# Attention and FFN in one kernel: lending two idle PSUM banks to the score tiles

## The chip, the cores and the metric

The kernel runs on one core of one Trainium2 chip. The metric is the device time of one execution in microseconds. The engines are named as in the profile: PE (TensorE), DVE (VectorE), ACT (ScalarE), POOL (GpSimd), SP (SyncE, which issues most DMAs here).

## The reference

Eight batches, eight heads, 576 positions, head size 64: causal attention with a learnt forgetting bias, then a feed-forward network with 2048 inner columns over the joined heads.

```python
scores = scale * np.matmul(q, k.transpose(0, 1, 3, 2))
s_pos = np.maximum(s, 0.0)
cum = np.cumsum(s_pos, axis=-1)
bias = -(cum[:, :, :, None] - cum[:, :, None, :])
scores = np.where(causal, -1000000000.0, scores + np.minimum(bias, 0.0))
scores = scores - np.max(scores, axis=-1, keepdims=True)
attn = np.exp(scores)
attn = attn / (np.sum(attn, axis=-1, keepdims=True) + 1e-09)
attn_out = np.matmul(attn, v)                  # (8, 8, 576, 64)
...
x = np.ascontiguousarray(attn_out.transpose(0, 2, 1, 3)).reshape(B * S, H * D)
h = x @ w_in
g = np.where(pos, h, np.where(neg, 0.0, (h + beta) ** 2 / (4.0 * beta)))
return (g @ w_out).astype(np.float32)
```

The weights come as 64-bit floats, which the kernel decodes itself on the chip.

## The kernel before, in words

Two streams of work share the engines. The first is attention. A job is a pair of heads and one half of the positions: half 0 has columns 0 to 319 (query tiles 0, 1 and 2), half 1 has columns 320 to 575 (query tiles 3 and 4). Eight jobs make a batch: four pairs in half 0, then four in half 1. A job has six score tiles. Each takes its PSUM bank from the pool `ps_s` (two banks), is written by one or two matmuls (line 407 for the first eight jobs, lines 412 and 413 later) and is emptied by one DVE instruction (line 418) that adds the mask and finds the extreme of each row. ACT then takes the exponential (line 429); once both heads of a query tile are there, `weights_t` normalises them into P, split into a high and a low 16-bit part, on ACT, POOL and DVE (lines 445 to 456), and a DMA issued by SP transposes them (line 457). `att_out` multiplies with V (line 475) into a tile px, which takes a bank of the same pool `ps_s`; ACT and DVE empty it into x (lines 486 and 487). Ahead of a job's scores stands a preparation of Q and K (lines 352 to 362) into buffers of which there is one each.

The second stream is the feed-forward network, half by half: a first half of 320 columns and a second of 256 for each batch, 16 steps each. `ffn_h` makes one tile h (line 530, twelve matmuls over the four pairs' x, two banks in `ps_h`), from which ACT, DVE and POOL make g in two parts (lines 542 to 557). `ffn_y` multiplies g with w_out into four accumulating tiles y of 128 output rows each (line 569, twelve matmuls a step), over all 16 steps. Each y tile has a bank of its own, tags y0 to y3 in `ps_y`; at the last step ACT scales it into a tile o and a DMA stores it (lines 583 and 584). So all eight banks are given away: two for scores and px, two for h, four for y. In a second half a y tile fills 256 of its bank's 512 columns.

At the start the weights are decoded, 16 chunks of w_in and 16 of w_out: the load (line 189), ACT and DVE instructions on the raw bits (lines 198 to 215) and a PE matmul that sums the exponents' bounds (line 203, tiles sum_wi in the banks y0 to y3, sum_wo in y0 and y1), then the scaling and splitting (lines 228 to 236). w_in comes with the first four attention jobs; w_out in the shadow of the first FFN half, whose h tiles are made ahead and whose y are made in two pairs of tiles (lines 652 to 658).

The program's order is written by the loop at its end, with attention six jobs ahead of the FFN later on. But the tile framework's scheduler places instructions anew when the kernel is built, by priorities and by its own estimate of when operands and buffers are free. A tile that finds no free buffer waits in that schedule too, and others are placed ahead of it. So the number of banks changes the order on every engine.

Of the kernel before, what the change touches and what calls it, by code (L numbers as in the profile page):

```python
# [9 lines left out]
F32 = mybir.dt.float32  # L10
# [4 lines left out]
AF = mybir.ActivationFunctionType  # L15
# [56 lines left out]
def attention_ffn(ctx: ExitStack, tc: tile.TileContext, qT, kT, vT, s, w_in, w_out, yT):  # L72
# [311 lines left out]

    vbs = {}

    ttr = [None]
    late = []

# [2 lines left out]
    def scores(n, i, hd, c0, c1):  # L392
# [8 lines left out]
            pbs[n, i].append(Pt)  # L401
            G.memset(Pt[:R, W:W + D], 0.0)
        Pt = pbs[n, i][hd]
        sc = ps_s.tile([P, 512], F32, tag="s", name=f"s{n}_{i}_{hd}_{c0}")
        j = jobs.index((n, i // 3))
        if j < F32_JOBS:
            T.matmul(
# [56 lines left out]
    def att_out(n, hf):  # L464

        b, p = n // NPAIR, n % NPAIR
        h_off, N, tiles = HALF[hf]
        nj = tiles[-1] + 1
        PT, VT = pts_.pop((n, hf)), vts[n]
        px = ps_s.tile([P, 512], F32, tag="s", name=f"px{n}_{hf}")  # L470
        steps = [(j, vl, pl) for j in range(nj) for vl, pl in ((0, 0), (1, 0), (0, 1))]
        for m, (j, vl, pl) in enumerate(steps):
            lo = max(0, j * P - h_off)
            for hd in range(2):
                T.matmul(  # L475
                    px[hd * D:(hd + 1) * D, lo:N],
                    VT[:, vl * NB + j, hd * D:(hd + 1) * D],
                    PT[:, 4 * j + 2 * hd + pl, lo:],
                    start=(m == 0), stop=(m == len(steps) - 1),
                )  # L480
        if p == 0:
            X[b, hf] = gp.tile([P, NKT, 2, N], F16, tag=f"x{hf}", bufs=2, name=f"x{b}_{hf}")
        x = X[b, hf]
        e = exs[b][:, p:p + 1]
        with tc.high_priority(offset=X_LEAD):
            A.activation(x[:, p, 0], px[:, :N], AF.Copy, scale=e)  # L486
            V.scalar_tensor_tensor(x[:, p, 1], px[:, :N], e, x[:, p, 0], ALU.mult, ALU.subtract)
# [68 lines left out]
                A.copy(g[:, 0], u)  # L556
            G.tensor_tensor(g[:, 1], u, g[:, 0], ALU.subtract)  # L557

    ys = {}

    def ffn_y(b, hf, ft, g, ms=tuple(range(NKT))):
        h_off, N, _ = HALF[hf]
        if ft == 0:
            for m in ms:
                ys[b, hf, m] = ps_y.tile([P, 512], F32, tag=f"y{m}", name=f"y{b}_{hf}_{m}")
        for m in ms:
            c0 = ft % 2 * 2 * P + m % 2 * P
            for n, (wl, gl) in enumerate(((0, 0), (1, 0), (0, 1))):
                T.matmul(  # L569
                    ys[b, hf, m][:, :N], WO[8 * (m // 2) + ft // 2][:, wl, c0:c0 + P], g[:, gl],  # L570
                    start=(ft == 0 and n == 0), stop=(ft == NFT - 1 and n == 2),
                )
        if ft == NFT - 1:
            last = (b, hf) == (B - 1, len(HALF) - 1)
            for m in ms:
                tag, bufs = ("u", 4) if last and m >= 2 else ("o", O_BUFS)
                o = gp.tile([P, N], F32, tag=tag, bufs=bufs, name=f"o{b}_{hf}_{m}")
                y = ys[b, hf, m][:, :N]
                with tc.high_priority(offset=FFN_LEAD):
                    if last and m % 2:  # L580
                        V.tensor_scalar(o, y, ysc[b][m // 2], None, ALU.mult)
                    else:
                        A.activation(o, y, AF.Copy, scale=ysc[b][m // 2])
                (nc.sync if last and m % 2 else nc.scalar).dma_start(
                    yT[m * P:(m + 1) * P, b * S + h_off:b * S + h_off + N], o
                )

    def ffn_step(s, k):

# [22 lines left out]
                batch_scales_v(0)  # L612
    while late:
        late.pop(0)()
    V.tensor_reduce(a_in, w1.bound, axis=AX, op=ALU.max)
    batch_scales(0)
    for c in range(3):
# [75 lines left out]
```

## Time and profile before

| what | value |
|---|---|
| median of three runs | 1115.04 us (1110.25 to 1115.35) |
| the profiled execution | 1111.73 us |
| its span, first to last instruction | 1109.9 us |
| PE busy | 1010.8 us, 91% |
| DVE, ACT, POOL busy | 76%, 65%, 61% |
| matmuls of h and of y | 3072 each |
| mean granted TensorE clock | 0.963 |

Lines of groups read: line, engine, operation, out<-in, shapes, count, then busy us, mean ns of one, and the idle time of the engine ahead of them with what ended it. Lines of stretches read: from and to in us, length, then busy us and count for PE, PE's weight loads, DVE, ACT and POOL, the granted clock, the DMA share and GB/s. Lines of waits read: who waits for whom, us in total, times, longest.

### The profile page before, as it was taken

The numbers are of one execution on the slowest core, as the hardware profiler recorded it, in microseconds if no ns is written. First come the engines' busy times: TensorE is split into PE (matmuls) and PEld (weight loads), VectorE is DVE, ScalarE is ACT, GpSimd is POOL, SyncE is SP. The second block draws the span as 40 slices with busy tenths as digits, with TensorE's granted clock in tenths as the row PEclk, the third lists the DMA queues.
The fourth block names the chain that finished last, engine by engine and source line by source line (L and its number), as shares of the span: only waits on it lengthen the run. The fifth ranks groups of instructions, "written<-read, shape, count | busy, mean of one in ns | idle before, by whom it ended". The sixth has DMA issues, their size and how long they took to land.

```text
span 1109.9 us, 25082 instructions
## 1 busy us (share of the span) xinstructions
PE 1010.8 (91%) x8495; PEld 774.9 (70%) x8496; DVE 846.3 (76%) x2325; ACT 725.8 (65%) x1703; POOL 679.0 (61%) x1173
## 2 busy tenths in 40 slices
PE   2456898799999999999999999899999999899998
PEld 1232466587768877777778877687778877787787
DVE  7887966688787877787778877787777887887533
ACT  4765985677567774867567765777576765777432
POOL 4782795775556764766467664666476665765522
PEclk9955999799999999999999999999999999999999
DMA  7876653786468663886468763877387763676300
GB/s 235 218 200 192 170 87 91 158 173 155 100 122 188 148 152 71 187 162 158 79 146 177 161 136 81 177 160 163 68 176 155 165 137 74 158 156 138 68 25 19
DMA packets 340775, 155.01 MB, mean 140 GB/s; under 512 B 290856, under 2 KB 322472, under 8 KB 340648
## 3 DMA queue, kind: packets, MB, share of 16 engines
q1 hardware_dynamic: 330944, 143.49, 59.6%
q10 hardware_dynamic: 9704, 9.93, 2.9%
q8 instruction: 67, 1.10, 0.4%
q14 instruction: 60, 0.49, 0.1%
HBM read 72.31 MB, written 9.73 MB: 74 GB/s over the span
## 4 chain that ended last, share of the span: by engine, by line
PE 61%; DVE 12%; POOL 8%; DMA 7%; issue 6%; ACT 5%; ACTq 0%; SPq 0%; DVEq 0%; POOLq 0%
PE y L569 25%; PE h L530 25%; PE px L475 4%; DMA pt<-pb 3%; PE s L412 3%; PE s L413 3%; DVE pb L456 2%; ACT u L542 2%; POOL pb L453 2%; POOL pb L450 2%; DVE p L418 1%; DVE Q L357 1%; DMA vt<-vb 1%; POOL vb L371 1%; DVE h L545 1%
## 5 line engine op out<-in xcount | busy, mean ns | idle before, releaser
L530 PE MATMUL h<-x,WI 128*128 128x256 f16 (+1 forms) x3072 | 463.9, 290 | 7.4 <-ACT x L486 3.4
L569 PE MATMUL y<-g,WO 128*128 128x256 f16 (+1 forms) x3072 | 457.8, 288 | 7.0 <-POOL g L557 5.3
L530 PEld LDWEIGHTS <-WI 128*128 128x128 f16 x3072 | 291.1, 99 | 97.0 <-issue 13.9
L569 PEld LDWEIGHTS <-WO 128*128 128x128 f16 x3072 | 288.1, 98 | 92.9 <-issue 13.8
L557 POOL TENSOR_TENSOR g<-u,g 128x320 f16<-128x320 f32 (+1 forms) x256 | 206.0, 805 | 152.1 <-ACT g L556 151.6
L429 ACT ACTIVATE p<-p,mn 64x64 f32<-64x64 f32 (+4 forms) x320 | 179.4, 561 | 142.7 <-DVE mn L418 122.2
L542 ACT ACTIVATE u<-h,ub,us 128x320 f32<-128x320 f32 (+1 forms) x256 | 149.1, 583 | 120.3 <-PE h L530 115.3
L545 DVE SCALAR_TENSOR_TENSOR h<-h,ws,u 128x320 f32<-128x320 f32 (+1 forms) x256 | 132.4, 517 | 110.6 <-ACT u L542 108.1
L450 POOL TENSOR_SCALAR pb<-p,rs 64x128 f16<-64x128 f32 (+4 forms) x160 | 95.3, 596 | 171.2 <-DVE rs L446 112.1
L453 POOL TENSOR_TENSOR pb<-p,pb 64x128 f16<-64x128 f32 (+4 forms) x160 | 173.9, 1087 | 9.5
L456 DVE SCALAR_TENSOR_TENSOR pb<-p,rs,pb 64x128 f16<-64x128 f32 (+4 forms) x160 | 134.6, 841 | 47.1 <-POOL pb L450 47.0
L418 DVE CUSTOM_DVE_ANT_0 p<-s,mask 64x64 f32<-64x64 f32 (+4 forms) x320 | 134.4, 420 | 31.3 <-PE s L413 23.0
L412 PE MATMUL s<-K,Q 128*64 128x64 f32 (+1 forms) x336 | 126.2, 377 | 16.0 <-DVE mn L418 10.9
L546 DVE SCALAR_TENSOR_TENSOR u<-u,r,h 128x320 f32<-128x320 f32 (+1 forms) x256 | 130.3, 509 | 6.8 <-DVE h L545 0.5
L451 ACT ACTIVATE p<-p,rs 64x64 f32<-64x64 f32 (+4 forms) x160 | 89.6, 560 | 51.3 <-DVE rs L446 49.4
L556 ACT CAST g<-u 128x320 f16<-128x320 f32 (+1 forms) x256 | 107.9, 421 | 10.3 <-DVE u L546 10.3
L413 PE MATMUL s<-K,Q 68*64 68x64 f32 (+1 forms) x336 | 102.8, 307 | 2.1 <-DMA K<-cumd 1.3
L452 POOL TENSOR_SCALAR pb<-p 64x128 f16<-64x128 f32 (+4 forms) x160 | 93.2, 583 | 11.9 <-ACT p L451 11.0
L475 PEld LDWEIGHTS <-vt 128*64 128x64 f16 x1536 | 73.4, 113 | 36.7 <-issue 30.2
L475 PE MATMUL px<-pt,vt 128*64 128x256 f16 (+3 forms) x1536 | 83.5, 259 | 13.3 <-DMA pt<-pb 8.7
L412 PEld LDWEIGHTS s<-K,Q 128*64 128x64 f32 (+1 forms) x336 | 61.5, 183 | 27.3 <-DVE mn L418 8.2
L413 PEld LDWEIGHTS s<-K,Q 68*64 68x64 f32 (+1 forms) x336 | 61.9, 184 | 5.8 <-issue 1.7
(105 smaller groups left out, 983.0 us busy)
## 6 DMA issues: line engine op xcount, KB each, us to landing
rk<-in_k_dram SPq DMA_DIRECT2D x56, 288.0 KB
v<-in_v_dram SPq DMA_DIRECT2D x32, 288.0 KB
rq<-in_q_dram SPq DMA_DIRECT2D x56, 160.0 KB
rk<-in_k_dram SPq DMA_DIRECT2D x56, 160.0 KB
wir<-in_moe_w_in_dram SPq DMA_DIRECT2D x16, 512.0 KB
wor<-in_moe_w_out_dram SPq DMA_DIRECT2D x16, 512.0 KB
rq<-in_q_dram SPq DMA_DIRECT2D x56, 128.0 KB
out_dram<-o ACTq DMA_DIRECT2D x32, 160.0 KB
```

What stands on the lines that cost most here:

```text
L412: T.matmul(sc[:R, :c1 - c0], Q1[:, hd, qo:qo + R], K1[:, hd, c0:c1], start=True, stop=False)
L413: T.matmul(sc[:R, :c1 - c0], Q2[:KC, hd, qo:qo + R], K2[:KC, hd, c0:c1], start=False, stop=True)
L418: ttr[0] = V.tensor_tensor_reduce(out=Pt[:R, c0:c1], in0=sc[:R, :c1 - c0], in1=mask[:R, mo:mo + c1 - c0], scale=-0.125 if j < F32_JOBS els ...
L429: A.activation(Pt[:R, :W], Pt[:R, :W], AF.Exp, bias=m2[:R], scale=-1.0, accum_out=sums[n, i][:R, hd:hd + 1])
L453: G.tensor_tensor(los[1], pw, his[1], ALU.subtract)
L456: V.scalar_tensor_tensor(los[0], pv, rs[:R, :1], his[0], ALU.mult, ALU.subtract)
L475: T.matmul(px[hd * D:(hd + 1) * D, lo:N], VT[:, vl * NB + j, hd * D:(hd + 1) * D], PT[:, 4 * j + 2 * hd + pl, lo:], start=(m == 0), stop=( ...
L530: T.matmul(h[:, :N], WI[4 * kt + ft // 4][:, wl, ft % 4 * P:(ft % 4 + 1) * P], x[:, kt, xl], start=(n == 0), stop=(n == 3 * NKT - 1),)
L542: first = A.activation(u, h[:, :N], AF.Relu, bias=ubi[b], scale=usc[b][:, fg:fg + 1]).ins
L545: V.scalar_tensor_tensor(h[:, :N], h[:, :N], wsc[b][:, fg:fg + 1], u, ALU.mult, ALU.max)
L557: G.tensor_tensor(g[:, 1], u, g[:, 0], ALU.subtract)
L569: T.matmul(ys[b, hf, m][:, :N], WO[8 * (m // 2) + ft // 2][:, wl, c0:c0 + P], g[:, gl], start=(ft == 0 and n == 0), stop=(ft == NFT - 1 an ...
```

## The change

In a second half, two y tiles of 256 columns share one bank: the tiles m = 0 and 1 lie in y0, the tiles 2 and 3 in y1. Only the first matmul of the first tile carries the start flag, and the second tile's first matmul is kept behind it (`issue_after`). At the end of the half one copy of 512 columns and one store of two tiles take the place of two each; in the very last half ACT copies the first bank and DVE the second.

The banks y2 and y3 are then free in second halves. A flag, `spare`, lends them to score and px tiles: every other such tile goes to `ps_y` under tag y2 or y3 in turn, the others to `ps_s` as before. The flag goes up when the decoding of w_in has been issued, down when the first half of a batch opens its tiles 2 and 3, and up again at the end of that half. So four banks serve the score and px tiles from there to the first half's second pair of y tiles, and in all second halves. The first halves' y tiles keep a bank each.

```diff
+    spare, turn = [False], [0]
+
+    def s_tile(name):
+        turn[0] += 1
+        if spare[0] and turn[0] % 2:
+            return ps_y.tile([P, 512], F32, tag=f"y{2 + turn[0] // 2 % 2}", name=name)
+        return ps_s.tile([P, 512], F32, tag="s", name=name)
...
-        sc = ps_s.tile([P, 512], F32, tag="s", name=f"s{n}_{i}_{hd}_{c0}")
+        sc = s_tile(f"s{n}_{i}_{hd}_{c0}")
...
-        px = ps_s.tile([P, 512], F32, tag="s", name=f"px{n}_{hf}")
+        px = s_tile(f"px{n}_{hf}")
...
+        w = 1 + hf
         if ft == 0:
-            for m in ms:
-                ys[b, hf, m] = ps_y.tile([P, 512], F32, tag=f"y{m}", name=f"y{b}_{hf}_{m}")
+            if ms[-1] == NKT - 1 and not hf:
+                spare[0] = False
+            for m in ms[::w]:
+                ys[b, hf, m // w] = ps_y.tile([P, 512], F32, tag=f"y{m // w}", name=f"y{b}_{hf}_{m}")
...
-                T.matmul(
-                    ys[b, hf, m][:, :N], WO[8 * (m // 2) + ft // 2][:, wl, c0:c0 + P], g[:, gl],
-                    start=(ft == 0 and n == 0), stop=(ft == NFT - 1 and n == 2),
-                )
+                opens = ft == 0 and n == 0
+                with tc.issue_after(opened[0]) if opens and m % w else ExitStack():
+                    opened[0] = T.matmul(
+                        ys[b, hf, m // w][:, m % w * N:(m % w + 1) * N],
+                        WO[8 * (m // 2) + ft // 2][:, wl, c0:c0 + P], g[:, gl],
+                        start=(opens and m % w == 0), stop=(ft == NFT - 1 and n == 2 and m % w == w - 1),
+                    ).ins
...
-                    if last and m % 2:
-                        V.tensor_scalar(o, y, ysc[b][m // 2], None, ALU.mult)
+                    if on_v:
+                        V.tensor_scalar(o.rearrange("p m n -> p (m n)"), y, scale, None, ALU.mult)
...
+            if ms[-1] == NKT - 1 and not hf:
+                spare[0] = True
...
     while late:
         late.pop(0)()
+    spare[0] = True
```

In the rows of instruction lists below, lines from 407 on carry the changed kernel's numbers where the list is of the change: 412 and 413 are 420 and 421 there, 475 is 483, 530 is 538, 569 is 582, 457 is 465. The names are s (scores: query tile, head, first column), px, h and y (half, then step or output tile), and a number for the buffer.

More of the change, by code (lines that the diff above doesn't have):

```diff
@@ L557, in g_split @@
             G.tensor_tensor(g[:, 1], u, g[:, 0], ALU.subtract)
-    ys = {}
+    ys, opened = {}, [None]
     def ffn_y(b, hf, ft, g, ms=tuple(range(NKT))):
         h_off, N, _ = HALF[hf]
+        w = 1 + hf
         if ft == 0:
-            for m in ms:
-                ys[b, hf, m] = ps_y.tile([P, 512], F32, tag=f"y{m}", name=f"y{b}_{hf}_{m}")
+            if ms[-1] == NKT - 1 and not hf:
+                spare[0] = False
+            for m in ms[::w]:
+                ys[b, hf, m // w] = ps_y.tile([P, 512], F32, tag=f"y{m // w}", name=f"y{b}_{hf}_{m}")
         for m in ms:
@@ L568, in ffn_y @@
             for n, (wl, gl) in enumerate(((0, 0), (1, 0), (0, 1))):
-                T.matmul(
-                    ys[b, hf, m][:, :N], WO[8 * (m // 2) + ft // 2][:, wl, c0:c0 + P], g[:, gl],
-                    start=(ft == 0 and n == 0), stop=(ft == NFT - 1 and n == 2),
-                )
+                opens = ft == 0 and n == 0
[5 more added lines that the diff above has]
+                    ).ins
         if ft == NFT - 1:
             last = (b, hf) == (B - 1, len(HALF) - 1)
[L575 to L578, printed above, removed]
+            for m in ms[::w]:
+                on_v = last and m > 0
+                o = gp.tile([P, w, N], F32, tag="o", bufs=O_BUFS, name=f"o{b}_{hf}_{m}")
+                y, scale = ys[b, hf, m // w][:, :w * N], ysc[b][m // 2]
                 with tc.high_priority(offset=FFN_LEAD):
-                    if last and m % 2:
-                        V.tensor_scalar(o, y, ysc[b][m // 2], None, ALU.mult)
-                    else:
-                        A.activation(o, y, AF.Copy, scale=ysc[b][m // 2])
-                (nc.sync if last and m % 2 else nc.scalar).dma_start(
-                    yT[m * P:(m + 1) * P, b * S + h_off:b * S + h_off + N], o
-                )
+                    if on_v:
+                        V.tensor_scalar(o.rearrange("p m n -> p (m n)"), y, scale, None, ALU.mult)
+                    else:
+                        A.activation(o.rearrange("p m n -> p (m n)"), y, AF.Copy, scale=scale)
+                (nc.sync if on_v else nc.scalar).dma_start(
+                    yT[m * P:(m + w) * P, b * S + h_off:b * S + h_off + N].rearrange("(m p) n -> p m n", p=P), o
+                )
+            if ms[-1] == NKT - 1 and not hf:
+                spare[0] = True
     def ffn_step(s, k):
```

## The prediction

> **What bounds the kernel now.** I read the page first, for the engine that is full and the stretches in which it is not.
>
> ```profile
> span 1109.9 us, 25082 instructions
> PE 1010.8 (91%) x8495; PEld 774.9 (70%) x8496; DVE 846.3 (76%) x2325; ACT 725.8 (65%) x1703; POOL 679.0 (61%) x1173
> ...
> PE   2456898799999999999999999899999999899998
> ...
> PEclk9955999799999999999999999999999999999999
> ```
>
> TensorE is full from the ninth slice on, so the end moves only by what PE loses: idle time and a lowered clock. To see where, I cut the start into stages and then took six stretches of 40 us, those in which a batch passes from its 320-column half to its 256-column half (the last row is their sum), and at last the time between them.
>
> ```profile
> 60.00:125.00 65.00, 44.23 (x186) 23.94 (x186) 54.30 (x147) 45.95 (x91) 36.95 (x58) 0.60 0.68 181
> 125.00:188.00 63.00, 59.57 (x432) 40.05 (x433) 45.31 (x118) 44.91 (x88) 46.37 (x58) 0.97 0.54 108
> 188.00:214.00 26.00, 15.08 (x124) 11.30 (x121) 17.34 (x55) 16.23 (x46) 18.71 (x35) 0.74 0.77 156
> 214.00:320.00 106.00, 105.63 (x930) 83.60 (x929) 84.18 (x233) 69.55 (x165) 67.83 (x115) 1.00 0.60 129
> ```
>
> ```profile
> 320.00:360.00 40.00, 36.63 (x338) 30.16 (x336) 31.77 (x103) 29.77 (x86) 27.65 (x65) 0.96 0.84 190
> ...
> 560.00:600.00 40.00, 37.44 (x342) 30.44 (x341) 31.11 (x98) 28.98 (x83) 28.63 (x62) 0.96 0.81 171
> ...
> 800.00:840.00 40.00, 37.51 (x338) 29.82 (x336) 30.46 (x101) 28.47 (x77) 25.25 (x53) 0.96 0.71 154
> ...
> sum 240.00, PE 222.45 PEld 180.26 DVE 187.32 ACT 174.57 POOL 161.22; mean PE 37.07 PEld 30.04 DVE 31.22 ACT 29.10 POOL 26.87
> ```
>
> ```profile
> sum 520.00, PE 516.33 PEld 403.29 DVE 400.29 ACT 333.83 POOL 303.45; mean PE 86.05 PEld 67.21 DVE 66.72 ACT 55.64 POOL 50.58
> ```
>
> The first numbers after a stretch are its length and PE's busy time; the one after the five engines is the granted clock. So PE idles 20.8 us in 60 to 125, when the weights are decoded, 3.4 in 125 to 188, 10.9 in 188 to 214, 17.6 in the six passages (240 − 222.45) and only 3.7 in the 520 us between them. The clock costs a little more: a stretch of 40 us at 0.96 lost 1.6 us, and three show it: 4.8. Behind 214 there are thus some 22 us to be had in the passages, and hardly anything elsewhere.
>
> What PE waits for comes from the list of waits, for 214 to 1080, and for 188 to 214:
>
> ```profile
> PE s L412 <- DVE mn L418: 7.0, 9, 1.9
> PE y L569 <- POOL g L557: 5.3, 7, 1.3
> PE s L412 <- DVE Q L357: 4.2, 5, 1.5
> ```
>
> ```profile
> PE px L475 <- DMA pt<-pb: 4.5, 1, 4.5
> PE s L412 <- DVE mn L418: 3.9, 3, 1.8
> ```
>
> "PE s <- DVE mn" is a score matmul whose bank is not free yet: VectorE's reduction at line 418 has to empty one of the two. That is 7.0 of the 22 us by name. The 4.5 us belong to one place, which the chain of waits tells step by step:
>
> ```profile
> 188.95 0.87 DVE rs L445
> ...
> 190.40 0.77 ACT p L451
> 191.24 1.28 POOL pb L452
> 192.59 2.18 POOL pb L453
> 194.91 5.58 DMA pt<-pb
> 200.62 2.77 PE px L475 x30
> ```
>
> From the last scores of batch 0's fourth pair to its px matmuls lie over 11 us of other engines' work, and PE has nothing else left to do: the half that comes next needs that px.
>
> **The change, part by part.** *More banks let scores move ahead.* The scheduler places a tile when its bank is free, so the list of the program is another one. First place: PE, where batch 0 goes over to its second half; px_1 on pt_1_1661 is the fourth pair's, h_1_0 the next half's first tile. Before:
>
> ```order
> L412 MATMUL s_1_1_0_1934<-K_1825,Q_1824 128x192
> L413 MATMUL s_1_1_0_1934<-K_90,Q_89 128x192
> L412 MATMUL s_2_0_0_1963<-K_1825,Q_1824 128x320
> L413 MATMUL s_2_0_0_1963<-K_90,Q_89 128x320
> L412 MATMUL s_2_1_0_1973<-K_1825,Q_1824 128x320
> L413 MATMUL s_2_1_0_1973<-K_90,Q_89 128x320
> L475 LDWEIGHTS vt_668
> L475 MATMUL px_1_1987<-pt_1_1661,vt_668 64x256
> ```
>
> After, the place where the last of those scores went, and what stands ahead of the px:
>
> ```order
> L582 MATMUL y_0_2_1752<-g_0_12_1390,WO_145 128x320
> L420 MATMUL s_2_1_0_1973<-K_1825,Q_1824 128x320
> L421 MATMUL s_2_1_0_1973<-K_90,Q_89 128x320
> L582 LDWEIGHTS WO_145
> L582 MATMUL y_0_3_1753<-g_0_12_1390,WO_145 128x320
> ```
>
> ```order
> L538 MATMUL h_1_0_2045<-x_1_1361,WI_122 128x256
> L538 LDWEIGHTS WI_114
> L538 MATMUL h_1_1_2077<-x_1_1361,WI_114 128x256
> L483 LDWEIGHTS vt_668
> L483 MATMUL px_1_1987<-pt_1_1661,vt_668 64x256
> ```
>
> The next job's scores moved from right ahead of the px into the first half's y matmuls. Between the pair's last scores (s_4_1_288) and its px stood 8 FFN matmuls, 30 of px and 12 of scores; now 111 FFN matmuls and the same others. An FFN matmul's price comes from the chain:
>
> ```profile
> 1099.46 1.31 PE y L569 x12
> ...
> 146.90 1.63 PE h L530 x12
> ```
>
> That is 0.109 us at 256 columns and 0.136 at 320: 103 matmuls more, most at 320, are some 14 us of cover for a chain of 11.7 (188.95 to 200.62). So the 4.5 us go, and the score waits beside them (3.9), since those scores stand among y matmuls now. Of 188 to 214 I take 10 us off: the 10.9 idle, less 2, and 1 for the clock (0.74 there). Bounds: 4 (the score waits alone) to 15 (all idle, and 4 for the clock).
>
> Second place: PE in the passages, here batch 4. Before, the second 320-column pair's scores:
>
> ```order
> L530 MATMUL h_1_1_10268<-x_1_9179,WI_126 128x256
> L412 MATMUL s_0_1_0_10041<-K_1825,Q_1824 64x64
> L413 MATMUL s_0_1_0_10041<-K_90,Q_89 64x64
> L412 MATMUL s_1_0_0_10077<-K_1825,Q_1824 128x192
> L413 MATMUL s_1_0_0_10077<-K_90,Q_89 128x192
> L530 LDWEIGHTS WI_126
> L530 MATMUL h_1_0_10222<-x_1_9179,WI_126 128x256
> ```
>
> After:
>
> ```order
> L582 MATMUL y_0_2_9315<-g_0_12_9955,WO_144 128x320
> L420 MATMUL s_0_1_0_10009<-K_1825,Q_1824 64x64
> L421 MATMUL s_0_1_0_10009<-K_90,Q_89 64x64
> L582 LDWEIGHTS WO_144
> L582 MATMUL y_0_3_9316<-g_0_12_9955,WO_144 128x320
> ```
>
> The pair's six score tiles stood among 27 FFN matmuls, 3.3 us; now among 73, about 9 us, and the px that the second half's first tile needs comes ahead of that half instead of behind its ninth matmul. It stays so in every later batch. What is late next: the third pair's six tiles stand closer (72 matmuls become 36, at least 3.9 us), but they have four banks; and the Q preparation (line 357, 4.2 us) is untouched. I keep 4.2 and some 4 more of the 22, so 14 go. Bounds: 7 (only the waits named mn) to 22.
>
> I weigh a rule against this. *By the rows above 7.0 us are put down to banks, the rest to other releasers.* The Trainium skill, "TensorE: Matmul & The Clock Gate", section "HAM oscillation — how this bites in real kernels", reports of its kernel that "adding PSUM double-buffering gave no further gain". By that, banks would return nothing here; what that makes of the time is the first rival.
>
> *The weights chain.* The same freedom puts attention ahead of w_out's decoding. Third place: SP's queue (wor = raw w_out chunks). Before:
>
> ```order
> L189 DMA wor_971<-in_moe_w_out_dram 128x2x512
> L189 DMA wor_978<-in_moe_w_out_dram 128x2x512
> L189 DMA wor_1155<-in_moe_w_out_dram 128x2x512
> L189 DMA wor_1162<-in_moe_w_out_dram 128x2x512
> L321 DMA QF_93<-in_q_dram 64x2x256
> L189 DMA wor_1209<-in_moe_w_out_dram 128x2x512
> ```
>
> After:
>
> ```order
> L189 DMA wor_971<-in_moe_w_out_dram 128x2x512
> L321 DMA QF_93<-in_q_dram 64x2x256
> L321 DMA KF_94<-in_k_dram 64x2x576
> L465 DMA_TRANSPOSE pt_1_944<-pb_3_945 128x16x128
> L189 DMA wor_978<-in_moe_w_out_dram 128x2x512
> ```
>
> Six of the 16 chunks now stand behind a P transpose whose input VectorE must finish, and three such transposes are ahead of the last chunk; it was one chunk and one transpose. On VectorE six more score reductions, two more P residuals and some small instructions stand ahead of the last decode (line 215):
>
> ```profile
> L418 DVE CUSTOM_DVE_ANT_0 p<-s,mask 128x448 f32<-128x448 f32 x64 | 39.4, 616 | 6.7 <-PE s L413 4.9 <-PE s L407 1.2 <-POOL pb L453 0.5
> L456 DVE SCALAR_TENSOR_TENSOR pb<-p,rs,pb 128x640 f16<-128x640 f32 x32 | 37.8, 1181 | 0.0
> L456 DVE SCALAR_TENSOR_TENSOR pb<-p,rs,pb 128x512 f16<-128x512 f32 x32 | 36.1, 1128 | 11.9 <-POOL pb L450 11.9
> L418 DVE CUSTOM_DVE_ANT_0 p<-s,mask,mn 128x288 f32<-128x288 f32 x64 | 32.4, 506 | 2.1 <-PE s L413 1.4 <-PE s L407 0.5
> ```
>
> Two at 0.62, four at about 0.5, 1.18 and 1.13 are 5.5 us; with the small ones about 7.5. VectorE idled 10.7 us in 60 to 125 and 17.7 in 125 to 188, so most of it can fill holes: I take +2. Bounds: −6 (PE's 20.8 idle us fill, and GpSimd's work comes earlier) to +8, unless the queue blocks: second rival.
>
> *Two tiles in a bank, the end.* Half as many copies of 512 columns instead of 256, off the path except at the end:
>
> ```profile
> 1101.91 4.09 PE L569 MATMUL y<-g,WO 128*128 128x256 f16 x36
> ...
> 1105.83 0.88 DVE L581 TENSOR_SCALAR o<-y,ys 128x256 f32<-128x256 f32 x2 [1.98 <-PE y L569]
> ```
>
> VectorE's two copies took 0.88 us, from before PE's end at 1106.0; one copy of 512 columns has the same elements but cannot start before the bank's last matmul, so +0.1 to +0.5, and a store of twice the bytes: I take +0.5 (0 to +1). The Trainium skill, "PSUM — Partial Sum Buffer", section "PSUM bank collisions raise a hardware error", says that no two engines may touch one bank's quadrant at once; so a copy waits for both tiles of its bank, not for its own. By that the price here is the upper end, +0.5 for the copy; no row of this trace has two tiles in a bank. Where the banks are handed back, y_0_2 and y_0_3 wait for a reduction (0.6 us), with over 3 us of other matmuls since the bank's last score in the list: nothing.
>
> The sum, against the profiled execution's own 1111.7 us (span 1109.9 and 1.8 around it; 3.3 under the median of the runs, 1115.04): 1111.7 − 10 − 14 + 2 + 0.5 = 1090.2.
>
> **The rivals.** *Banks were not the bound.* Two thirds of the passages' waits bear other names, and the transposed DMA remains. Then the next wait comes up where one is removed and only little is left: 1111.7 − 4 + 2 = 1110, no change. Against it: the list moves the consumer, not the bank alone. 0.11.
>
> *The weights come late.* Two transposes more stand ahead of the last wor load. If each holds SP's queue for its whole chain, 10.1 us from line 451 to the landing by the rows above (190.40 to 194.91 + 5.58), the last decode comes 20.2 + 7.5 = 27.7 us later, and with it PE's last sum matmul of the weights, now at
>
> ```profile
> 138.74 0.39 PE sum_wo L203
> ```
>
> The first half's y must follow it. With the 188 to 214 stall gone (−10) and only the named bank waits in the passages (−7), the time is 1111.7 + 27.7 − 10 − 7 = 1122.4: slower. It decides once that matmul is more than 17 us later, at 156. Against it: VectorE's holes, and ten chunks whose place in the queue is unchanged. 0.06.
>
> *Half of it.* 188 to 214 improves by its score waits alone (4), the passages by 7, the weights cost 2: 1103. It is the forecast's weak end, 0.13.
>
> **How the numbers follow.** My forecast, 1090, has 0.70. Its own ends: −15 −22 −6 gives 1069, −4 −7 +8 +1 gives 1109.7; ends that need every term at its bound together are unlikely, so I cut to 1076 below and 1106 above, which leaves out the rivals that are not faster and about 3 in 100 below. A measurement of this kernel tells about 0.5% from no change: faster is under 1109.5, against the median. Forecast and weak end give faster 0.83, the first rival 0.11 same, the second 0.06 slower.
>
> **What would show it.** Right: the px of batch 0's fourth pair without a wait of microseconds, PE idle in each passage under 1.5 us (2.9 now), the clock at 1.00 in the stretches of 0.96, the waits "PE s <- DVE mn" behind 214 near nothing. Wrong: the last sum_wo matmul behind 150, or passages as idle as now under other releasers' names (POOL g, DVE Q), or a new idle stretch where the third 320-column pair's scores stand close.

## The result and the profile after

The changed kernel takes 1107.82 us (median of 8 runs, 1101.69 to 1114.57); the kernel before, run beside it, 1113.54 us (8 runs, 1109.87 to 1115.79). The ratio is 0.9947, with a 95% interval of 0.9924 to 0.9971: faster by about half a per cent, 5.7 us. The forecast was 1090, with a range up to 1106, so the time lies 17.8 us above the forecast and outside the range.

The profiled execution of the changed kernel took 1112.35 us, one of its longer ones, so it says where time went rather than how much. Its page:

```profile
span 1110.6 us, 24982 instructions
PE 1012.2 (91%) x8495; PEld 781.6 (70%) x8496; DVE 851.8 (77%) x2324; ACT 725.1 (65%) x1688; POOL 692.8 (62%) x1173
...
PE   2466899899999999999999899999999999989998
...
PEclk9955899999999999999999999999999999999999
```

PE's seventh and eighth slices, 8 and 7 before, are 9 and 8 now. The stages of the start, in the columns of the prediction (length, PE, PEld, DVE, ACT, POOL, granted clock, DMA share, GB/s):

```profile
60.00:125.00 65.00, 45.27 (x165) 24.06 (x167) 52.77 (x152) 41.64 (x86) 37.85 (x62) 0.55 0.74 187
125.00:188.00 63.00, 60.24 (x439) 40.34 (x438) 49.84 (x130) 51.87 (x103) 53.60 (x65) 0.96 0.55 114
188.00:214.00 26.00, 21.44 (x197) 17.62 (x196) 18.61 (x54) 17.11 (x47) 18.35 (x37) 0.93 0.80 178
214.00:320.00 106.00, 102.85 (x897) 80.44 (x896) 85.31 (x232) 70.19 (x162) 67.46 (x114) 0.98 0.65 129
```

In 188 to 214 PE is busy 21.44 us instead of 15.08, with 197 matmul records instead of 124. Then the sums over the six passages, and over the 520 us between them:

```profile
sum 240.00, PE 232.70 PEld 191.52 DVE 200.02 ACT 183.57 POOL 172.78; mean PE 38.78 PEld 31.92 DVE 33.34 ACT 30.60 POOL 28.80
```

```profile
sum 520.00, PE 502.12 PEld 395.11 DVE 388.59 ACT 320.13 POOL 298.66; mean PE 83.69 PEld 65.85 DVE 64.77 ACT 53.35 POOL 49.78
```

This is the main part of the miss. The passages did gain, most of the 14 us that were forecast: PE's busy time rose from 222.45 to 232.70, 10.3 us. But between them it fell from 516.33 to 502.12, 14.2 us. The waits of 214 to 1080 name what came:

```profile
PE px L483 <- DMA pt<-pb: 17.8, 10, 2.9
PE s L420 <- DVE x L495: 2.2, 4, 1.5
...
PE s L420 <- DVE Q L357: 1.1, 1, 1.1
...
PE y L582 <- POOL g L565: 0.8, 3, 0.5
```

The bank waits named mn ("PE s <- DVE mn", 7.0 us before) are gone, and Q (4.2) and g (5.3) have shrunk to 1.1 and 0.8. In their place PE stands 17.8 us before px matmuls whose transposed P has not landed (0.8 us before). Of these, 11.7 us fall on one px of a batch, that of the first pair in the 256-column half's attention (up to 2.9 us in each of the batches 2 to 7), and 5.4 on the fourth 320-column pair's (batches 1 to 3).

**Why P is late.** One such place in full, that first pair in batch 4. SP's queue and PE:

```profile
619.36 2.95 SPq L465 DMA_TRANSPOSE pt<-pb  x1
```

```profile
607.99 0.30 PE L421 MATMUL s<-K,Q 68*128 68x288 f32 x1
...
625.53 1.87 PE L483 MATMUL px<-pt,vt 128*64 128x256 f16 x15 [2.73 <-DMA pt<-pb]
```

The pair's last score ends at 608.3, its transpose is issued 11.1 us later, and px starts another 6.2 us on, after 2.73 us of idling. Between the score and the transpose stands first VectorE:

```profile
607.97 1.15 DVE L464 SCALAR_TENSOR_TENSOR pb<-p,rs,pb 128x512 f16<-128x512 f32 x1 [0.33 <-POOL pb L458]
609.04 0.47 DVE L554 SCALAR_TENSOR_TENSOR u<-u,r,h 128x256 f32<-128x256 f32 x1
609.44 0.51 DVE L426 CUSTOM_DVE_ANT_0 p<-s,mask,mn 128x288 f32<-128x288 f32 x1
...
609.87 0.45 DVE L426 CUSTOM_DVE_ANT_0 p<-s,mask 128x288 f32<-128x288 f32 x1
...
610.47 0.52 DVE L426 CUSTOM_DVE_ANT_0 p<-s,mask,mn 128x288 f32<-128x288 f32 x1
```

Three score tiles that PE wrote between 605.5 and 608.3 lie in their banks until VectorE takes them at 609.4 to 611.0, one right after the other: ahead of them stand the residual of the tile before (1.15 us, after a wait of 0.33 for GpSimd's line 458) and a step of the FFN. So the last score and its reduction are 2.5 us apart, from start to start. In the kernel before they are 0.7 us apart, and the transpose comes 8.2 us after the end of the score (619.63 to 627.79):

```profile
619.34 0.29 PE L413 MATMUL s<-K,Q 68*128 68x288 f32 x1
```

```profile
620.02 0.51 DVE L418 CUSTOM_DVE_ANT_0 p<-s,mask,mn 128x288 f32<-128x288 f32 x1
```

```profile
627.79 2.93 SPq L457 DMA_TRANSPOSE pt<-pb  x1
```

Of the 2.9 us by which the transpose is later, 1.8 thus arise ahead of the reduction. The rest arises behind it: the tile's exponential stands behind ScalarE's preparation of Q and K and starts 2.6 us after the reduction's start (610.47 to 613.08), where it was 1.3 (620.02 to 621.36).

So two more banks let PE hand in its scores early, but the engines behind them don't work faster: a wait of PE for a bank became a wait of the scores in a bank, and PE met the same delay at px. Worked out from the same rows for six jobs of batch 4 (us from the end of the job's last score matmul to the issue of its last transpose, and from there to px):

| | 320 columns: pair 1 | 2 | 3 | 4 | 256 columns: pair 1 | 2 |
|---|---|---|---|---|---|---|
| before | 7.5, 7.5 | 11.1, 4.8 | 8.0, 6.2 | 9.3, 5.4 | 8.2, 7.2 | 8.6, 8.8 |
| after | 7.4, 8.0 | 8.0, 4.1 | 12.6, 3.9 | 11.4, 3.4 | 11.1, 6.2 | 13.2, 9.1 |

Four of the six chains to the transpose are 2 to 4.6 us longer, one is 3 us shorter. The FFN matmuls that PE's list holds between last score and px are 68, 123, 104, 106, 104 and 103 before, and 99, 89, 121, 101, 100 and 116 after. For the four longer chains the cover thus grew by 17 and 13 matmuls in two cases, at the prediction's 0.109 to 0.136 us each at most 2.3 us, and shrank by 5 and 4 in the others: less than the chains grew.

### The profile page after: what moved, and what is told of

Its sections match the earlier page's. It is cut to its first block, busy times and chain, and to the rows that moved or that the text cites. A ratio compares the mean times of both kernels' runs of the same rounds, so it can differ in the third digit from the quotient of the medians.

```text
span 1110.6 us, 24982 instructions
## 1 busy us (share of the span) xinstructions
PE 1012.2 (91%) x8495; PEld 781.6 (70%) x8496; DVE 851.8 (77%) x2324; ACT 725.1 (65%) x1688; POOL 692.8 (62%) x1173
## 5 line engine op out<-in xcount | busy, mean ns | idle before, releaser
L582 PE MATMUL y<-g,WO 128*128 128x256 f16 (+1 forms) x3072 | 450.5, 288 | 4.9 <-ACT WO L228 2.2
L538 PE MATMUL h<-x,WI 128*128 128x256 f16 (+1 forms) x3072 | 447.1, 290 | 6.0 <-DVE u L554 4.7
L538 PEld LDWEIGHTS <-WI 128*128 128x128 f16 x3072 | 294.4, 99 | 94.5 <-issue 12.5
L458 POOL TENSOR_SCALAR pb<-p,rs 64x128 f16<-64x128 f32 (+4 forms) x160 | 100.3, 628 | 159.1 <-DVE rs L454 97.0
L464 DVE SCALAR_TENSOR_TENSOR pb<-p,rs,pb 64x128 f16<-64x128 f32 (+4 forms) x160 | 131.0, 819 | 22.1 <-POOL pb L458 21.2
L420 PE MATMUL s<-K,Q 128*128 128x448 f32 (+2 forms) x336 | 117.9, 361 | 5.0 <-DVE x L495 2.2
L564 ACT CAST g<-u 128x320 f16<-128x320 f32 (+1 forms) x256 | 107.9, 422 | 11.2 <-DVE u L554 10.9
L460 POOL TENSOR_SCALAR pb<-p 64x128 f16<-64x128 f32 (+4 forms) x160 | 99.2, 620 | 17.3 <-ACT p L459 15.5
L421 PE MATMUL s<-K,Q 68*64 68x64 f32 (+1 forms) x336 | 96.1, 306 | 1.3 <-POOL K L360 0.7
L420 PEld LDWEIGHTS s<-K,Q 128*128 128x128 f32 (+1 forms) x336 | 59.8, 181 | 13.8 <-DVE x L495 2.2
L360 DVE TENSOR_TENSOR K<-rk,K 64x1152 fp32r<-64x1152 f32 (+1 forms) x52 | 64.9, 1248 | 2.0 <-ACT K L355 0.3
```

What stands on the lines that cost most here:

```text
L420: T.matmul(sc[:R, :c1 - c0], Q1[:, hd, qo:qo + R], K1[:, hd, c0:c1], start=True, stop=False)
L464: V.scalar_tensor_tensor(los[0], pv, rs[:R, :1], his[0], ALU.mult, ALU.subtract)
L538: T.matmul(h[:, :N], WI[4 * kt + ft // 4][:, wl, ft % 4 * P:(ft % 4 + 1) * P], x[:, kt, xl], start=(n == 0), stop=(n == 3 * NKT - 1),)
L582: opened[0] = T.matmul(ys[b, hf, m // w][:, m % w * N:(m % w + 1) * N], WO[8 * (m // 2) + ft // 2][:, wl, c0:c0 + P], g[:, gl], start=(ope ...
```

## The experiments

The kernel before ran again beside each set of runs (medians 1112.12 to 1113.23, and 1113.54 beside the changed kernel), and the ratios are to that. Differences between kernels of different sets, in us, carry about 1 us of that. First, the parts.

**The parts of the change, one at a time.** The changed kernel with the lending at the start alone:

```
             if ms[-1] == NKT - 1 and not hf:
-                spare[0] = True
```

> The changed kernel with its lending kept only at the start: from the first weight's decoding to the first half's second pair; in all later 256-column halves scores and px have their own two banks again. Theory 1 (lost to the transposed P): the change gains at the start, by the named px and score waits of 188 to 214 us less the later weights; in the passages it gains some 10 us and loses all of it again behind them, because the px come up sooner after their last scores than the chain exp, residual, transpose can follow, so that PE waits for the transposed P. Then this kernel stands with the changed one: 5 to 8 us below the kernel before, and the waits 'px <- DMA pt' behind 214 fall from 17.8 us to under 8. Theory 2 (the passages did gain, the start lost): slower than or equal to the kernel before. Theory 3 (any list of this kernel is held by the engines that make P, so the banks do nothing anywhere): within 2 us of the kernel before.

Measured: 1115.39, ratio 1.002 (1.000 to 1.004). Theory 1 wanted 5 to 8 us less and theory 3 a time within 2 us. Theory 2 (slower or equal) fits by the number, but not by its reason, since the start did gain (PE is 21.19 us busy in 188 to 214, where the kernel before had 15.08). What was lost lies behind 320 us, under the old names, all longer than before (5.3, 7.0 and 4.2 us):

```profile
PE y L582 <- POOL g L565: 9.7, 12, 2.4
PE s L420 <- DVE mn L426: 7.8, 6, 3.3
PE s L420 <- DVE Q L357: 7.1, 5, 2.6
```

The counterpart, lending in the second halves alone:

```
     while late:
         late.pop(0)()
-    spare[0] = True
```

> The changed kernel with its lending kept only in the later 256-column halves, not at the start. Theory 1: within 3 us of the kernel before, since what the passages gain (PE 10 us busier in the six stretches of 40 us) goes to waits for the transposed P in the stretches between (PE 14 us idler there). Theory 2: 5 to 14 us faster than the kernel before. Theory 3: within 2 us.

Measured: 1117.23, ratio 1.0035 (1.0017 to 1.0052): theory 1's "within 3 us" is missed by 2, but the forecast's gain of 5 to 14 us is excluded. In 214 to 1080 its px wait 15.7 us for P, as in the changed kernel.

Both parts alone are slower than the kernel before, and together they are faster, so something that both kernels contain must cost time: two y tiles to a bank. The changed kernel without any lending (both of the edits above, and the line that sets it to False):

> The changed kernel without any lending: two y tiles to a bank in the 256-column halves, the other two banks idle. From 320 us on it has the list of the kernel that lends at the start only, which lost some 10 us more behind 320 us than the kernel before (its waits for POOL g, for Q and for the score banks are longer). Theory 1, as now amended (two tiles to a bank cost about 10 us by themselves, each of the two lendings gives some 8 back): 6 to 11 us slower than the kernel before. If instead lending at the start is what disturbs the later order, it is within 3 us of the kernel before.

Measured: 1122.61, ratio 1.0084 (1.0069 to 1.0099), 9.6 us slower, as the amended theory said. Its waits in 214 to 1080:

```profile
PE y L582 <- POOL g L565: 10.4, 14, 1.4
PE s L420 <- DVE mn L426: 9.3, 5, 3.3
```

So by medians, all but the first from different sets of runs: two tiles to a bank +9.6, lending at the start −7.2 (start_only against pairs_only), lending in the second halves −7.6 (the changed kernel against start_only) or −5.4 (second_only against pairs_only). That leaves the last question of the sum: the start alone, on the kernel before, without shared banks.

```
+            if ms[-1] == NKT - 1:
+                spare[0] = False
             for m in ms:
...
+    spare[0] = True
     V.tensor_reduce(a_in, w1.bound, axis=AX, op=ALU.max)
```

with the changed kernel's s_tile for scores and px.

> The kernel before with lending at the start alone: scores and px have the banks of y_2 and y_3 from the first weight's decoding to the first half's second pair; no two y tiles share a bank, and from batch 1 on the list is the kernel before's. Two pairs of kernels that differ in the start alone gave 9.4 us (changed kernel against second_only) and 7.2 us (start_only against pairs_only). If that part stands by itself: 6 to 10 us below the kernel before, and thus at or below the changed kernel, whose second halves then bring nothing or a loss. If it needs the rest: within 4 us of the kernel before.

Measured: 1107.57, ratio 0.9954 (0.9939 to 0.9970), 5.7 us faster: 0.3 short of the 6 to 10 expected, and the same time as the changed kernel. Its stages:

```profile
188.00:214.00 26.00, 21.38 (x193) 17.25 (x191) 18.89 (x56) 17.26 (x47) 19.56 (x40) 0.87 0.82 173
...
320.00:1080.00 760.00, 737.77 (x6530) 583.76 (x6531) 586.20 (x1630) 506.97 (x1230) 461.43 (x833) 1.00 0.64 136
```

Behind 330 us the instructions of every engine come in the order of the kernel before, so that this pair isolates the start. The start holds the whole gain of the change. The edits to the second halves, taken together, bring nothing.

**What the wait for P is worth.** px of batches 1 to 7 read a slice of w_in instead of P, in the changed kernel and in the kernel before, with px held behind the h matmul after which they are written (the attention of these batches is thus left out of the result):

```
-                    PT[:, 4 * j + 2 * hd + pl, lo:],
+                    WI[4 * j % 16 + 2 * hd + pl][:, 1, lo:N] if b else PT[:, 4 * j + 2 * hd + pl, lo:],
```

> The changed kernel, but from batch 1 on the px matmuls multiply V by a slice of the decoded w_in (its low halves) instead of the transposed P: as many matmuls, of the same shapes, nearly in the same order, and all P tiles are still made and transposed; only the wait for their landing is gone (the attention of batches 1 to 7 is thus left out of the result). Theory 1: most of the 17.8 us of 'px <- DMA pt' come back: 10 to 16 us below the changed kernel, and PE behind 214 us idles under 10 us. Theory 3 (another wait, for Q, u, g or a bank, ends just behind that of P): less than 4 us below the changed kernel.

> The same edit on the kernel before: px of batches 1 to 7 multiply V by a slice of w_in instead of the transposed P (so that attention is left out of the result), the matmuls and nearly their order are kept. Its trace shows 'px <- DMA pt' for 4.2 us outside the one wait at 200 us. Theory 1: 2 to 5 us below the kernel before, so that the changed kernel gains at least 8 us more from the same edit. Theory 3: within 2 us of the kernel before, and no more gain than in the changed kernel.

Measured: 1095.67, ratio 0.9841 (0.9819 to 0.9863), 12.2 us below the changed kernel; and 1111.55, ratio 0.9989 (0.9971 to 1.0006), 0.6 below the kernel before, less than the 2 to 5 expected. The waits left in the first (214 to 1080) are "PE y <- POOL g", 8.1 us, and smaller ones:

```profile
PE y L583 <- POOL g L566: 8.1, 16, 1.1
PE s L421 <- ACT x L494: 3.4, 5, 0.9
```

So in the changed kernel the wait for P is worth some 12 us, and in the kernel before it was worth next to nothing. Theory 3 falls. Two reservations: PE still idles 16.7 us in 320 to 1080 (760 − 743.26), not under 10 as theory 1 had it, and the list isn't quite the changed kernel's, since for instance the third 320-column pair's px stands 76 FFN matmuls behind its last score instead of 121.

**Giving P more time.** A job's slot in the program has eight units, and px stood in the last unit of the slot behind its job's. The px written two units later (LATE_K = 1, px_later) or four (LATE_K = 3, px_later3), and taken out of the old place from batch 1 on:

```
+        if j > 2 * NPAIR + 1 and k == LATE_K and j <= len(jobs) + 1:
+            with tc.issue_after(last_h[0]):
+                att_out(*jobs[j - 2])
```

> The changed kernel with the px matmuls put two slots of the program later, behind the h matmuls that stand there; from their last scores to px lie then 18.8 us of matmuls instead of 14.1 for the first pair of a 320-column half's attention, 16.0 instead of 14.2 for the fourth 256-column... in short two of the eight jobs of a batch gain 2 to 5 us of cover, the others under 1. Theory 1 (PE comes to px too early): those two waits of a batch go, some 4 of the 17.8 us: 2 to 6 us below the changed kernel. Theory 4 (GpSimd makes the P tiles too late, since with four banks two tiles come to it at once, and work that is only listed later on PE waits as well): within 2 us of the changed kernel.

> The same with px two slots and two units later: 14.2 becomes 19.5 us for the last of the four jobs, 12.3 becomes 13.5 for the second, and 5 to 8 us more for those of the other half; but the h matmuls of the next half then stand closer behind the last px. Theory 1: 4 to 9 us below the changed kernel. Theory 4: within 3 us of it, or slower where h now waits for x.

Measured: 1114.47, ratio 1.0007 (0.9990 to 1.0024), and 1154.98, ratio 1.0376 (1.0357 to 1.0394). The first is over 6 us slower than the changed kernel, which neither theory had (2 to 6 us faster, or within 2 us); the second is 47 us slower, where theory 4 had left room for "slower where h now waits for x" (PE's waits "PE h <- ACT x" are 5.8 us there, a small part of the 47). Theory 1 in its plain form (PE merely comes too early) falls. In the first of them the wait for P is gone and another has its place:

```profile
PE y L587 <- POOL g L570: 19.3, 18, 2.7
PE h L543 <- DVE u L559: 3.0, 8, 0.5
...
PE px L484 <- DMA pt<-pb: 0.7, 3, 0.3
```

**Relieving GpSimd.** One step of the 384-column P tile goes from GpSimd to VectorE:

```
-        G.tensor_tensor(los[1], pw, his[1], ALU.subtract)
+        (V if i == 2 else G).tensor_tensor(los[1], pw, his[1], ALU.subtract)
```

> The changed kernel with one step of a P tile moved from GpSimd to VectorE: the second residual of the 384-column tile (0.91 us on GpSimd, up to 5 us behind its first step there because another tile, a g and memsets stand in between). PE's list behind 320 us is almost unchanged. Theory 4: P lands 1 to 4 us sooner in the three jobs of a batch that wait, the waits 'px <- DMA pt' fall from 17.8 to under 10 us: 4 to 9 us below the changed kernel. Theory 1 in its plain form (the chain has its own length, and PE is early): the chain shortens by under 1 us per job, at most 3 us in all.

Measured: 1096.79, ratio 0.9855 (0.9836 to 0.9874): 11 us below the changed kernel, 16.2 below the kernel before, the fastest whole kernel of the study. From batch 3 on, the places of scores and px among PE's FFN matmuls are the changed kernel's, but for one px of a batch, six matmuls later, and one score tile, two matmuls earlier; the order on VectorE and GpSimd differs more. The waits in 214 to 1080:

```profile
PE px L483 <- DMA pt<-pb: 11.9, 12, 1.7
PE y L582 <- POOL g L565: 2.3, 4, 1.0
```

At the place shown above the last score and its reduction are now 1.2 us apart instead of 2.5 (start to start). VectorE is ahead there: both 448-column reductions now stand before the 384-column residual of line 464, and that takes 0.61 us where it took 1.13 (at 603.74 us of the changed kernel):

```profile
604.70 0.29 PE L421 MATMUL s<-K,Q 68*128 68x288 f32 x1
```

```profile
600.68 0.61 DVE L464 SCALAR_TENSOR_TENSOR pb<-p,rs,pb 128x384 f16<-128x384 f32 x1
...
601.70 0.56 DVE L461 TENSOR_TENSOR pb<-p,pb 128x384 f16<-128x384 f32 x1
...
603.81 1.15 DVE L464 SCALAR_TENSOR_TENSOR pb<-p,rs,pb 128x512 f16<-128x512 f32 x1
...
605.92 0.52 DVE L426 CUSTOM_DVE_ANT_0 p<-s,mask,mn 128x288 f32<-128x288 f32 x1
```

The waits for P fell less than expected (11.9, not under 10); the time fell more than expected. In 320 to 1080 PE idles 16.6 us, 25.2 in the changed kernel.

Then the same work given back to GpSimd, with the result of VectorE kept:

```
+        if i == 2:
+            z = ap.tile([P, 3, P], F16, tag="z", bufs=1, name=f"z{n}")
+            G.tensor_tensor(z, pw, his[1], ALU.subtract)
```

> v_res, with the work given back to GpSimd: VectorE's residual still goes into the P tile, and GpSimd computes the same residual a second time into a scratch tile that nothing reads. PE's list behind 140 us is that of v_res. If it is GpSimd's load that makes P and g late, the 11 us of v_res are lost again: within 4 us of the changed kernel. If the gain of v_res came from P no longer waiting in GpSimd's queue, or from the list, it keeps 7 us or more of them. cut_res, which freed GpSimd and gained nothing because its px came up 1 to 3 us sooner in the list, speaks for the second.

Measured: 1111.27, ratio 0.9985 (0.9969 to 1.0000): 14.5 us are lost again, and the time is within the 4 us of the changed kernel that was expected if GpSimd's load is the cause. Behind 262 us PE's list is that of v_res but for five or six h matmuls a batch, and behind 330 us VectorE and ScalarE have the same instructions in the same order; in the profiled executions, 10.4 of the lost 14.0 us lie between the end of batch 0 and that of batch 6. Nothing reads that scratch tile, so the cause is the step on GpSimd. Its waits, and how busy the engines are in 320 to 1080, with v_res's row behind:

```profile
PE px L486 <- DMA pt<-pb: 14.5, 13, 2.4
PE y L585 <- POOL g L568: 3.6, 7, 0.9
PE s L420 <- DVE mn L426: 2.0, 5, 1.3
```

```profile
sum 760.00, PE 736.74 PEld 588.58 DVE 608.44 ACT 506.66 POOL 486.30; mean PE 736.74 PEld 588.58 DVE 608.44 ACT 506.66 POOL 486.30
```

```profile
sum 760.00, PE 743.42 PEld 596.69 DVE 601.17 ACT 508.30 POOL 456.74; mean PE 743.42 PEld 596.69 DVE 601.17 ACT 508.30 POOL 456.74
```

GpSimd is busy 64% of that time with the step and 60% without. It is nowhere near full, and still one step of about 1 us for each of 32 tiles costs 14.5 us. The step can do that in two ways. P steps, g and memsets stand in one queue, and what comes late there holds VectorE and then SP. And VectorE itself is slower beside it: with the same instructions it is busy 608.44 us instead of 601.17, most of all in the residual of that tile (v_res, then v_res_load, in 320 to 1080):

```profile
L464 DVE SCALAR_TENSOR_TENSOR pb<-p,rs,pb 128x384 f16<-128x384 f32 x24 | 15.4, 641 | 2.2 <-POOL pb L458 2.2
L467 DVE SCALAR_TENSOR_TENSOR pb<-p,rs,pb 128x384 f16<-128x384 f32 x24 | 20.9, 870 | 1.4 <-POOL pb L458 1.4
```

No run tells the two apart.

The step left out instead of moved:

```
+        if i == 2 and n >= NPAIR:
+            A.copy(los[1], pw)
+        else:
             G.tensor_tensor(los[1], pw, his[1], ALU.subtract)
```

> The changed kernel, with the second residual of the 384-column P tile left out from batch 1 on: ScalarE writes a plain copy of P in its place (so that P's low half of one head is not computed), which depends on ScalarE's own earlier step only. GpSimd is freed as in v_res, but VectorE gets nothing to do. Theory 4 (with four banks, GpSimd's P steps are what PE waits for): 8 to 15 us below the changed kernel, at or below v_res. If v_res was faster for another reason (its list), no faster than 4 us.

Measured: 1108.38, ratio 0.9958 (0.9942 to 0.9974), the changed kernel's time: the expectation of 8 to 15 us is missed, though GpSimd has the same relief as in v_res and VectorE less to do (ScalarE has the copies instead, 12.2 us in 320 to 1080).

```profile
PE px L486 <- DMA pt<-pb: 22.5, 19, 3.1
```

What differs is PE's list. The scheduler places px when it reckons P to have landed; with a shorter chain it moved the third 320-column pair's px from 121 to 97 FFN matmuls behind the last score, and the second 256-column pair's from 116 to 93. In v_res those places are 121 and 116. The waits agree: 11.2 of the 22.5 us now fall on the third 320-column pair's px, which hardly waited before (0.7 us). So the relief was spent in advance.

**The same move with two banks.** The kernel before with the step on VectorE (the line of v_res) and with the step left out (the lines of cut_res), and pairs_only with the one and with the other:

> The kernel before with the second residual of the 384-column P tile on VectorE instead of GpSimd, nothing else. Theory 4 as it now stands (the four banks brought scores early, two P tiles then come to GpSimd at once, and the wait that GpSimd causes took the place of the bank waits): with two banks the tiles come one by one and the waits are those for banks, so the same move gives much less than the 11 us it gave in the changed kernel: 0 to 4 us. If GpSimd is too slow in any list of this kernel (theory 5), the move gives about as much here, 8 to 12 us, and the four banks add only what pairs and lending add by themselves, some 6 us.

> The same on the kernel before (that residual left out from batch 1 on, a copy by ScalarE in its place). The kernel before with the step on VectorE was 21.6 us slower. If VectorE's additional work did that (a score reduction stands behind the moved step, and with two banks the next score waits for it), this kernel, where VectorE gets none, is within 5 us of the kernel before. If the shifted list of the two-bank kernel did it (its third job's scores lie 3 us later in PE's list, and this kernel has the same list), it is over 10 us slower as well. A gain of over 8 us would say that GpSimd bounds the two-bank kernel too.

> The kernel with two y tiles to a bank and no lending, with the same step on VectorE. Without it this kernel was 9.6 us slower than the kernel before, with waits for POOL g of 10.4 us and for score banks of 9.3 us. Theory 4: the bank waits stay, and the gain is at most 5 us. Theory 5: 8 to 12 us below pairs_only, the POOL g waits under 4 us.

> The same on the kernel with two y tiles to a bank and no lending. That kernel was 9.6 us slower than the kernel before; behind 320 us this one has the kernel before's list again, but for the places of px. If the list and not the shared banks cost the 9.6 us, it stands within 4 us of the kernel before; if the shared banks cost them, it stays 6 or more above.

Measured: 1134.05, ratio 1.0188 (1.0163 to 1.0214); 1126.47, ratio 1.0127 (1.0100 to 1.0153); 1138.25, ratio 1.0222 (1.0197 to 1.0248); 1114.62, ratio 1.0019 (1.0002 to 1.0037). With two banks the move costs 21.6 us on the kernel before and 15.6 on pairs_only, which neither theory 4 (0 to 4 and at most 5 gained) nor theory 5 (8 to 12) had. VectorE's additional work is not the main cause, since the kernel that gives VectorE none loses 13.5 as well. In both the list has moved: the first 320-column pair's px stands 32 to 44 FFN matmuls behind its last score in five of six cases (batches 4 to 6 of the two kernels), 68 in the kernel before, and the waits for Q have grown from 4.2 to 9.9 us in the one and to 5.4 in the other. That speaks for the list, but no run holds it fixed, so why the loss is so large stays open. The last of the four points the same way for the shared banks: it has them too, has nearly the kernel before's score places, and is only 1.7 us above that kernel instead of 9.6. It leaves a GpSimd step out as well, though, so the two causes are not cleanly apart.

**More of it.** The same step of two tile sizes on VectorE, and v_res with px two units later, the edit of px_later. The first two edits, against v_res:

```
-        (V if i == 2 else G).tensor_tensor(los[1], pw, his[1], ALU.subtract)
+        (V if i in (1, 2) else G).tensor_tensor(los[1], pw, his[1], ALU.subtract)
...
+        (V if i in (2, 4) else G).tensor_tensor(los[1], pw, his[1], ALU.subtract)
```

> The changed kernel with that step on VectorE for the 256-column tile too (1.10 us more off GpSimd for each of 32 tiles, and VectorE, now 79% busy, gets them). Both theories: the waits that GpSimd still causes ('px <- DMA pt' 11.9 us, POOL g 2.3) shrink, but VectorE's own queue stands behind the moved step while that waits for GpSimd's half: within 5 us of v_res, to either side; over 3 us faster would say that GpSimd is still the next limit, slower that VectorE has become it.

> The changed kernel with that step on VectorE for the 384-column and the 640-column tile. The px of the 640-column tiles wait hardly anywhere (their last transpose lies 5 to 20 us before px), so nothing is gained there by sooner P; GpSimd's g get free. Within 3 us of v_res if those tiles are covered as the trace says; slower if VectorE's 64 further microseconds of such work stand ahead of score reductions.

> v_res with px two slots later, as in px_later, where the waits 'px <- DMA pt' went and waits for GpSimd's g came in their place (19.3 us). Theory 4: with GpSimd relieved, those are shorter: 8 us or more below px_later; against v_res, where 11.9 us of px waits are left, from 5 us faster to 3 us slower. If the waits for g had another cause than GpSimd's load, it stays within 4 us of px_later.

Measured: 1116.78, ratio 1.0034 (1.0021 to 1.0047); 1119.57, ratio 1.0064 (1.0042 to 1.0086); 1118.71, ratio 1.0059 (1.0039 to 1.0079). Each lost 20 us or more against v_res. The first and the third expectation are missed; the second allowed for "slower", if VectorE's work stood ahead of score reductions, but no run shows that this was the reason. In the first the list moved the third 320-column pair's px nearer again (98 FFN matmuls behind its last score), as in cut_res; in the second "PE s <- DVE Q" is back with 8.6 us. In the third the waits for g are 13.4 us in spite of the relief (19.3 without it), so those have a cause besides this step, and it stays open.

## Why the prediction was wrong

- **The step that failed is the −14 for the six passages.** The prediction asked "what is late next" and answered with the Q preparation and "some 4 more of the 22". The waits that it removed did go, and the passages gained (10.3 us of PE's time, and the clock 1.00 in all six instead of 0.96 in three). Three of its four signs of being right came true (no wait at batch 0's fourth px, none named mn, the clock at 1.00), and the fourth in part: PE idles under 1.5 us in three of the six passages. None of its signs of being wrong did. But the next thing late was P, tens of microseconds behind each passage, where the prediction did not look: its row for the stretches between ("PE 516.33" of 520) was read as safe because it was full. Measured for the part itself: lending in the second halves −5 to −8 us, sharing the banks that it needs +9.6, and both edits together nothing (b_start against the changed kernel, 1107.57 and 1107.82).
- **A term was missing**: two tiles to a bank were costed at the end of the program only (+0.5). In the list that they make they cost 9.6 us; whether by the list or by the bank is open.
- **The start was about right.** 188 to 214 was put at −10 and the weights at +2, together −8. Three pairs of kernels that differ in the start alone give −5.7, −7.2 and −9.4 us (the last two by medians of two sets of runs). PE's busy time in 188 to 214 rose by 6.4 us. No px in that stage of the changed kernel waits for P any more (in b_start one does, for 2.2 us); PE's waits there are:

```profile
PE h L538 <- DVE u L554: 3.8, 2, 3.0
PE s L421 <- POOL K L360: 0.7, 1, 0.7
```

- **The weights came late, but not by much.** The last sum matmul of w_out starts 4.5 us later than at 138.74, short of the 150 that was named as the sign of being wrong and of the second rival's 156. What part of the 4.5 us reached the end is not measured apart from the start's sum:

```profile
143.28 0.39 PE L203 MATMUL sum_wo<-WO,ones 128*128 128x512 bf16 x1 [0.64 <-DVE WO L199]
```

- **The end**: VectorE's last copy, now of 512 columns, starts when PE ends (1106.51), and the span ends 4.1 us behind PE (1106.49 to 1110.6), where it was 3.9 (1106.0 to 1109.9). That is +0.2 for the +0.5.
- **The first rival had the mechanism** ("the transposed DMA remains", the next wait comes up where one is removed) and got 0.11. It left 4 us of gain in all, and so 1110; what it missed is the start. The rule set beside it, "adding PSUM double-buffering gave no further gain" (the Trainium skill, "TensorE: Matmul & The Clock Gate", section "HAM oscillation — how this bites in real kernels"), holds here for the second halves only in their sum, where lending gave 5 to 8 us and the shared banks took 9.6, and not for the start, where b_start shows 5.7 us.
- **The range** had no case in which the start gains and the passages give nothing. By its own terms that is 1111.7 − 10 + 2 + 0.5 = 1104, and 1107.5 against the median instead of the one profiled execution. That this is within 1 us of the time that was measured is partly luck, since the start gave less than its −8.

## What to carry to other kernels

More buffers between two engines let the first run ahead; they help to the end only if what is made behind them is in time as well, so follow the data past the freed wait to its consumer, here px, and compare the cover there with the chain. Where a scheduler writes the list, every edit moves it: cost the list that results, and compare kernels whose lists agree (b_start and the kernel before, v_res and v_res_load) before an engine is blamed. Split a change into its parts on the chip: here one half of it, b_start, is the whole gain, and in the second halves four banks paid off only together with one step less on GpSimd.

## What was not expected of the hardware

- The 128x384 residual, the same operation and types, takes 0.91 us on GpSimd in the changed kernel's row below and 0.99 on average of the 24 in 320 to 1080; on VectorE (v_res, line 461) it takes 0.56 in the row above and 0.55 on average. The Trainium skill, "GPSIMD Engine Reference", section "When to use GPSIMD", puts two-input operations there at about twice VectorE's time; here it is 1.6 to 1.8 times.

```profile
472.62 0.91 POOL L461 TENSOR_TENSOR pb<-p,pb 128x384 f16<-128x384 f32 x1
```

- In the weights' stage the granted clock was 0.60 in the profiled execution of the kernel before and 1.00 in that of second_only, which lends nothing there either. PE has 186 matmul records in both and its busy time differed little (44.23 and 42.80 us of 65). The start of second_only was no faster for it: its last sum matmul of w_out starts at 139.84, that of the kernel before at 138.74. So the clock did not set the pace of that stage.

```profile
60.00:125.00 65.00, 42.80 (x186) 22.62 (x186) 55.28 (x144) 44.28 (x89) 35.06 (x55) 1.00 0.67 180
```
